# Sinkhorn block attention followed by a four-expert layer on one core: keys mixed and transposed in one matmul, attention output kept on chip, instruction order written by hand

## The chip, the cores and the metric

The kernel runs on one core of one Trainium2 chip. The time is the device time of one execution in microseconds (us). Of the kernel before there are three runs: 533.26, 534.28 and 534.55 us, median 534.28 us. One further execution was taken with the hardware profiler, and all durations below are from it.

## What is computed

There are 4 batches of 8 heads, 768 positions and a head dimension of 64. Positions form 8 blocks of 96. For each head an 8x8 matrix P is normalised five times by rows and columns. Keys and values are then mixed block by block with P, each block of queries attends to the mixed block at the same place, and all heads of a position, joined to 512 numbers, go through four experts whose outputs are weighted and added.

```python
for _ in range(5):
    P = exp(P - max(P));  P = P / sum(P, axis=-1);  P = P / sum(P, axis=-2)
k_sorted = einsum('bhij,bhjcd->bhicd', P, k_blocks)      # the same for v
attn = softmax(scale * q_block @ k_sorted_block.T) @ v_sorted_block
x = attn as [4*768, 512]
for e in range(4):
    out += p[:, e:e+1] * (relu(x @ w1[e]) @ w2[e])       # w1 512x1024, w2 1024x512
```

## The kernel before

All matmul operands are float16; inputs are cast from float32 by the loads. "Tile" means a named buffer, and two heads that share the 128 partitions are called a pair: there are 16 pairs, 4 to a batch.

*Start.* SyncE loads `sort_net` into `sn` (L89), and ScalarE and VectorE normalise it (L92 to L103). The 8x8 matrices go to DRAM and come back rearranged (`p_dram` L106, `rhsP` L110). A small matmul (L112) and a mask (L119) make from them a block-diagonal 128x128 matrix `bd` for 16 heads at a time.

*Mixing.* GpSimd loads all of k and v (`mixsrc`, L130). 48 matmuls of 512 columns with `bd` mix them (L140), VectorE copies each result out (L142, tiles `mo`, four buffers), and SyncE stores it to `ks_dram` or `vs_dram` (L143).

*Queries.* 32 loads of 96 KB (L156, issued by GpSimd), 6 transposes for each pair (L161) and a copy (L163) give `qT`.

*Attention, pair by pair* (L241 to L313). Mixed keys are read back from DRAM (L245), transposed (L250) and copied (L252); mixed values are read back (L260). Scores of two heads come from 16 matmuls (L276), ScalarE takes their exponential in halves of 384 columns (L283), 16 matmuls with the exponential as weights apply them to the values (L297; a column of ones gives the sum), VectorE divides (L303, L304), and SyncE stores the result to `x_dram` (L311).

*Experts* (`moe_block`, L184 to L234), batch by batch. The batch's 768 rows are read back from `x_dram` (L186), transposed (L191) and copied by ScalarE to `xT` (L192). For each expert, 16 results `ps_h` of 384 columns (4 matmuls each, L201) go through a Relu (L207), and then 6 results `ps_o` of 512 columns (8 matmuls each, L214) are scaled and added by VectorE (L224, L229). The last expert's sums are stored (L234).

*What sets the order.* The program gives pairs and blocks in order, with `moe_block(b-1)` behind the last pair of batch b, and a scheduler that knows dependences and buffers decides how they stand on each engine. PSUM is two pools of four one-bank buffers, `psA` for attention and `psM` for experts. GpSimd keeps eight loads in flight.

Of the kernel before, what the change touches and what calls it, by code (L numbers as in the profile page):

```python
# [9 lines left out]
F32 = mybir.dt.float32  # L11
F16 = mybir.dt.float16
AF = mybir.ActivationFunctionType
ALU = mybir.AluOpType


@with_exitstack
def kernel(
# [15 lines left out]
    NBLK = sort_net.shape[-1]  # L34
    BLK = S // NBLK
# [6 lines left out]
    NCH = (BLK * D) // 512  # L42
    NKC = Dm // P
    NFC = FF // P
    NTC = S // P
    NPAIR = GH // 2
    NPB = H // 2
    NSUB = S // P
    NHALF = 2
    HBL = S // NHALF  # L50

    consts = ctx.enter_context(tc.tile_pool(name="consts", bufs=1))
    dramp = ctx.enter_context(tc.tile_pool(name="dramp", bufs=1, space=bass.MemoryType.DRAM))
    small = ctx.enter_context(tc.tile_pool(name="small", bufs=1))
# [3 lines left out]
    def psa(shape, dtype, name):  # L58
        return psA.tile(shape, dtype, tag="ps", name=name)

    def psm(shape, dtype, name):
        return psM.tile(shape, dtype, tag="ps", name=name)

    p_dram = dramp.tile([GH, NBLK, NBLK], F16, name="p_dram")
    ks_dram = dramp.tile([GH, S, D], F16, name="ks_dram")
    vs_dram = dramp.tile([GH, S, D], F16, name="vs_dram")
    x_dram = dramp.tile([B, S, H, D], F16, name="x_dram")

    ident = consts.tile([P, P], F16, name="ident")
    make_identity(nc, ident)  # L70
    lhsT8 = consts.tile([NBLK, 16, NBLK], F16, name="lhsT8")
    nc.gpsimd.memset(lhsT8[:], 0.0)
    nc.gpsimd.affine_select(
        out=lhsT8[:], in_=lhsT8[:], compare_op=ALU.not_equal, fill=1.0,
        base=0, pattern=[[0, 16], [1, NBLK]], channel_multiplier=-1,
    )
    bdmask = consts.tile([P, 16, NBLK], F16, name="bdmask")
    nc.gpsimd.memset(bdmask[:], 1.0)
    nc.gpsimd.affine_select(
        out=bdmask[:], in_=bdmask[:], compare_op=ALU.is_ge, fill=0.0,  # L80
        base=7, pattern=[[8, 16], [0, NBLK]], channel_multiplier=-1,
    )
    nc.gpsimd.affine_select(
        out=bdmask[:], in_=bdmask[:], compare_op=ALU.is_ge, fill=0.0,
        base=0, pattern=[[-8, 16], [0, NBLK]], channel_multiplier=1,
    )

    sn = small.tile([GH, NBLK, NBLK], F32, name="sn")
    nc.sync.dma_start(sn[:], sort_net.rearrange("b h i j -> (b h) i j"))  # L89
    srow = small.tile([GH, NBLK, 1], F32, name="srow")  # L90
    scol = small.tile([GH, NBLK, 1], F32, name="scol")
    for it in range(5):  # L92
        nc.scalar.activation(sn[:], sn[:], AF.Exp, bias=0.0, scale=1.0)
        nc.vector.tensor_reduce(srow[:], sn[:], mybir.AxisListType.X, ALU.add)
        nc.vector.reciprocal(srow[:], srow[:])
        nc.vector.tensor_tensor(sn[:], sn[:], srow[:].broadcast_to([GH, NBLK, NBLK]), ALU.mult)
        nc.vector.tensor_reduce(scol[:], sn[:].rearrange("p i j -> p j i"), mybir.AxisListType.X, ALU.add)
        nc.vector.reciprocal(scol[:], scol[:])
        nc.vector.tensor_tensor(
            sn[:], sn[:],  # L100
            scol[:].rearrange("p j o -> p o j").broadcast_to([GH, NBLK, NBLK]),
            ALU.mult,
        )  # L103
    sn16 = small.tile([GH, NBLK, NBLK], F16, name="sn16")
    nc.vector.tensor_copy(sn16[:], sn[:])
    nc.scalar.dma_start(p_dram[:], sn16[:])  # L106
    bdts = []
    for m in range(2):
        rhsP = small.tile([NBLK, 16, NBLK], F16, name=f"rhsP_{m}")
        nc.scalar.dma_start(rhsP[:], p_dram[ds(16 * m, 16)].rearrange("g i j -> j g i"))  # L110
        ps_bd = psa([P, P], F32, f"ps_bd_{m}")
        nc.tensor.matmul(  # L112
            ps_bd[:],
            lhsT8.rearrange("jp g j -> jp (g j)"),
            rhsP.rearrange("jp g i -> jp (g i)"),
            start=True, stop=True,
        )
        bdt = small.tile([P, P], F16, name=f"bd_{m}")
        nc.vector.tensor_tensor(bdt[:], ps_bd[:], bdmask.rearrange("p g i -> p (g i)"), ALU.mult)  # L119
        bdts.append(bdt)  # L120

    qtp = ctx.enter_context(tc.tile_pool(name="qtp", bufs=NPAIR))
    wpool = ctx.enter_context(tc.tile_pool(name="wpool", bufs=1))

    with tc.tile_pool(name="mixsrc", bufs=1) as mixsrc, tc.tile_pool(name="mixout", bufs=4) as mixout:
        srcs = {}
        for m in range(2):
            for (tin, nm) in ((k, "k"), (v, "v")):
                src = mixsrc.tile([P, NCH, 512], F16, name=f"mixsrc_{nm}_{m}", tag=f"mixsrc_{nm}_{m}")
                nc.gpsimd.dma_start(  # L130
                    src.rearrange("p ch c -> p (ch c)"),
                    tin.rearrange("b h (j c) d -> (b h j) (c d)", j=NBLK)[ds(P * m, P), :],
                )
                srcs[(nm, m)] = src
        for m in range(2):
            for (tdr, nm) in ((ks_dram, "k"), (vs_dram, "v")):
                src = srcs[(nm, m)]
                for ch in range(NCH):
                    ps_mx = psa([P, 512], F32, f"ps_mx_{m}_{nm}_{ch}")
                    nc.tensor.matmul(ps_mx[:], bdts[m][:], src[:, ch, :], start=True, stop=True)  # L140
                    mo = mixout.tile([P, 512], F16, name=f"mo_{nm}_{m}_{ch}", tag="mo")
                    nc.vector.tensor_copy(mo[:], ps_mx[:])  # L142
                    nc.sync.dma_start(  # L143
                        tdr.rearrange("g (i ch cc) d -> (g i) ch cc d", ch=NCH, cc=8)[
                            ds(P * m, P), ch, :, :
                        ],
                        mo.rearrange("p (cc d) -> p cc d", cc=8),
                    )

        qTs = []  # L150
        with tc.tile_pool(name="qnp", bufs=4) as qnp:
            for pr in range(NPAIR):
                b, h2 = divmod(pr, NPB)
                q_nat = qnp.tile([P, NTC, 2, D], F16, name=f"q_nat_{pr}", tag="q_nat")
                for hh in range(2):
                    nc.gpsimd.dma_start(  # L156
                        q_nat[:, :, hh, :], q[b, 2 * h2 + hh].rearrange("(t p) d -> p t d", p=P)
                    )
                ps_qT = psa([P, NTC, P], F16, f"ps_qT_{pr}")
                for t in range(NTC):  # L160
                    nc.tensor.transpose(ps_qT[:, t, :], q_nat[:, t, :, :], ident[:])  # L161
                qT = qtp.tile([P, NTC, P], F16, name=f"qT_{pr}", tag="qT")
                nc.vector.tensor_copy(qT[:], ps_qT[:])  # L163
                qTs.append(qT.rearrange("dd t c -> dd (t c)"))
# [194 lines left out]
```

## Time and profile before

| what | value |
|---|---|
| profiled execution, first to last instruction | 532.5 us |
| median of three runs | 534.28 us |
| TensorE matmul busy | 417.9 us (78%) |
| VectorE busy | 160.8 us (30%) |
| ScalarE busy | 163.4 us (31%) |
| DMA moved | 43.50 MB in 125983 packets, 107008 of them under 512 bytes |
| first expert matmul on the chain that ended last | 171.85 us |
| end of that chain's last matmul | 528.39 us |

The profiled execution lies 1.8 us below the median of the runs. PE is TensorE, PEld its weight loads, DVE VectorE, ACT ScalarE, POOL GpSimd, SP SyncE; a "q" behind the name is the engine's own queue of DMA issues. A row of a group of instructions gives line, engine, operation, tiles written and read, shapes, count, then busy time, the mean duration of one in ns, and the engine's idle time before them with what ended it. A matmul's own duration holds the time until its result is written, so that matmuls in a stream overlap: what one costs in a stream is read from many of them, time by count.

### The profile page before, as it was taken

The numbers are of one execution on the slowest core, as the hardware profiler recorded it, in microseconds if no ns is written. First come the engines' busy times: TensorE is split into PE (matmuls) and PEld (weight loads), VectorE is DVE, ScalarE is ACT, GpSimd is POOL, SyncE is SP. The second block draws the span as 40 slices with busy tenths as digits, with TensorE's granted clock in tenths as the row PEclk, the third lists the DMA queues.
The fourth block names the chain that finished last, engine by engine and source line by source line (L and its number), as shares of the span: only waits on it lengthen the run. The fifth ranks groups of instructions, "written<-read, shape, count | busy, mean of one in ns | idle before, by whom it ended". The sixth has DMA issues, their size and how long they took to land.

```text
span 532.5 us, 6716 instructions
## 1 busy us (share of the span) xinstructions
PE 417.9 (78%) x2642; PEld 227.0 (43%) x2642; DVE 160.8 (30%) x341; ACT 163.4 (31%) x342; POOL 41.2 (8%) x87
## 2 busy tenths in 40 slices
PE   0003331464578999999999999999999999999996
PEld 0000000023466655545565554566555455455552
DVE  4102332583454331131533213153221311212213
ACT  1000000000135713514562351456235145252250
POOL 5114000029200000000000000000000000000000
PEclk9999999995555999999999999999999999999999
DMA  7999999879978900000571000144100012000003
GB/s 137 219 157 151 234 228 230 192 183 130 78 120 164 173 6 0 1 1 28 143 127 47 0 1 0 41 119 70 42 0 2 0 41 80 0 1 0 1 0 119
DMA packets 125983, 43.50 MB, mean 82 GB/s; under 512 B 107008, under 2 KB 120320, under 8 KB 125440
## 3 DMA queue, kind: packets, MB, share of 16 engines
q0 software_dynamic: 31936, 17.83, 26.9%
q1 hardware_dynamic: 85312, 15.80, 16.0%
q10 hardware_dynamic: 8704, 9.45, 6.0%
q8 instruction: 21, 0.34, 0.3%
q14 instruction: 10, 0.08, 0.0%
HBM read 45.15 MB, written 15.73 MB: 114 GB/s over the span
## 4 chain that ended last, share of the span: by engine, by line
PE 68%; ACT 3%; DMA 2%; DVE 1%; issue 0%; ACTq 0%
PE ps_o L214 31%; PE ps_h L201 31%; PE ps_av L297 2%; ACT ET L283 2%; DMA xnat<-x_dram 1%; PE ps_sT L276 1%; PE ps_kT L250 1%; PE ps_xT L191 1%; ACT xT L192 1%; DMA q_nat<-in_q_dram 1%; DVE kT L252 1%; DMA x_dram<-xsl 0%; PE ps_qT L161 0%; ACT hT L207 0%; DVE xsl L304 0%
## 5 line engine op out<-in xcount | busy, mean ns | idle before, releaser
L207 ACT ACTIVATE hT<-ps_h 128x384 f16<-128x384 f32 x256 | 124.5, 492 | 166.2 <-PE ps_h L201 164.1
L201 PE MATMUL ps_h<-xT,w 128*128 128x384 f16 x1024 | 173.9, 326 | 0.6 <-ACT xT L192 0.5
L214 PE MATMUL ps_o<-w,hT 128*128 128x512 f16 x768 | 168.4, 379 | 0.0
L201 PEld LDWEIGHTS <-w 128*128 128x128 f16 x1024 | 99.2, 98 | 66.2 <-issue 1.5
L214 PEld LDWEIGHTS <-hT 128*128 128x128 f16 x768 | 75.1, 98 | 89.0
L229 DVE SCALAR_TENSOR_TENSOR oacc<-ps_o,p_sb,oacc 128x512 f32<-128x512 f32 x72 | 54.1, 751 | 195.1 <-PE ps_o L214 195.1
L283 ACT ACTIVATE ET<-ps_sT 96x384 f16<-96x384 f32 x64 | 26.1, 492 | 154.1 <-PE ps_sT L276 154.0
L112 PE MATMUL ps_bd<-rhsP,lhsT 8*128 8x128 f16 x2 | 0.5, 259 | 46.7 <-DMA rhsP<-p_dram 46.7
L140 PEld LDWEIGHTS <-bd 128*128 128x128 f16 x48 | 5.1, 109 | 66.6 <-issue 66.6
L156 POOL DMA_DIRECT2D q_nat<-in_q_dram x32 | 26.3, 862 | 91.8 <-PE ps_qT L161 66.1
L224 DVE TENSOR_SCALAR oacc<-ps_o,p_sb 128x512 f32<-128x512 f32 x24 | 18.0, 751 | 45.5 <-PE ps_o L214 45.5
L140 PE MATMUL ps_mx_v<-mixsrc_v,bd 128*128 128x512 f16 x24 | 14.0, 585 | 20.2 <-DVE mo_v L142 14.4
L140 PE MATMUL ps_mx_k<-mixsrc_k,bd 128*128 128x512 f16 x24 | 13.1, 595 | 20.5 <-DVE mo_v L142 10.4
L304 DVE TENSOR_TENSOR xsl<-ps_av,rz 96x256 f16<-96x256 f32 x64 | 24.8, 408 | 0.9 <-DVE rz L303 0.3
L297 PE MATMUL ps_av<-vs,ET 96*96 96x65 f16 x256 | 21.3, 234 | 4.7 <-ACT ET L283 4.6
L142 DVE CAST mo_v<-ps_mx_v 128x512 f16<-128x512 f32 x24 | 15.9, 689 | 23.2 <-DMA vs_dram<-mo_v 18.2
L297 PEld LDWEIGHTS <-ET 96*96 96x96 f16 x256 | 18.3, 150 | 9.8 <-ACT ET L283 8.8
L161 PE MATMUL ps_qT<-ident,q_nat 128*128 128x128 f16 x96 | 12.0, 299 | 13.1 <-DMA q_nat<-in_q_dram 10.9
L261 POOL MEMSET vs<- 96x8 f16 x32 | 4.1, 133 | 217.9 <-PE ps_av L297 195.6
L142 DVE CAST mo_k<-ps_mx_k 128x512 f16<-128x512 f32 x24 | 15.7, 687 | 14.6 <-DMA ks_dram<-mo_k 13.1
L303 DVE RECIPROCAL rz<-ps_av 96x4 f32<-96x4 f32 x64 | 11.3, 176 | 28.4 <-PE ps_av L297 26.8
L192 ACT COPY xT<-ps_xT 128x768 f16<-128x768 f16 x16 | 11.9, 816 | 23.8 <-PE ps_xT L191 23.7
(39 smaller groups left out, 101.8 us busy)
## 6 DMA issues: line engine op xcount, KB each, us to landing
w<-in_moe_w_dram POOLq DMA_DIRECT2D x8, 1024.0 KB, 29.7
out_dram<-oacc ACTq DMA_DIRECT2D x24, 256.0 KB, 2.0
mixsrc_k<-in_k_dram POOLq DMA_DIRECT2D x2, 1536.0 KB, 17.8
mixsrc_v<-in_v_dram POOLq DMA_DIRECT2D x2, 1536.0 KB, 24.7
q_nat<-in_q_dram POOLq DMA_DIRECT2D x32, 96.0 KB, 3.9
ks_dram<-mo_k SPq DMA_DIRECT2D x24, 128.0 KB, 5.8
vs_dram<-mo_v SPq DMA_DIRECT2D x24, 128.0 KB, 3.0
ks_nat<-ks_dram SPq DMA_DIRECT2D x32, 96.0 KB, 2.9
```

The lines of the kernel that those rows point to most:

```text
L140: nc.tensor.matmul(ps_mx[:], bdts[m][:], src[:, ch, :], start=True, stop=True)
L142: nc.vector.tensor_copy(mo[:], ps_mx[:])
L156: nc.gpsimd.dma_start(q_nat[:, :, hh, :], q[b, 2 * h2 + hh].rearrange("(t p) d -> p t d", p=P))
L192: nc.scalar.copy(xT[:, u, :], ps_xT[:])
L201: nc.tensor.matmul(ps_h[:], w1sb[e][:, kc, ds(fc * P, P)], xT[:, kc, ds(nh * HBL, HBL)], start=(kc == 0), stop=(kc == NKC - 1),)
L207: nc.scalar.activation(hT[:, fc, ds(nh * HBL, HBL)], ps_h[:], AF.Relu, bias=0.0, scale=1.0)
L214: nc.tensor.matmul(ps_o[:], hT[:, fc, ds(ns * P, P)], w2sb[e][:, fc, :], start=(fc == 0), stop=(fc == NFC - 1),)
L224: nc.vector.tensor_scalar(out=oacc[:], in0=ps_o[:], scalar1=pcol, scalar2=None, op0=ALU.mult)
L229: nc.vector.scalar_tensor_tensor(out=oacc[:], in0=ps_o[:], scalar=pcol, op0=ALU.mult, in1=oacc[:], op1=ALU.add,)
L283: nc.scalar.activation(ETs[hh][:, ds(half * 4, 4), :], pshh[hh][:, :, 0:96], AF.Exp, bias=0.0, scale=SCALE,)
L297: nc.tensor.matmul(ps_av[:, ii, 0:D + 1], ET[:, i, :], vs_sb[:, i, 0:D + 1], start=True, stop=True,)
L304: nc.vector.tensor_tensor(xsl[:, ds(half * 4, 4), :], ps_av[:, :, 0:D], rz[:, ds(half * 4, 4), :].broadcast_to([96, 4, D]), ALU.mult,)
```

## The change

*Layout.* A partition holds 6 consecutive positions of a head (`load_natural`, rows of 6x64 numbers), so that 16 partitions make one block of 96. k, v and q of a batch are three tiles, loaded for 4 or 8 heads at a time. The order of positions inside a block is the same everywhere and is put back by the store of the output.

*Mixing.* The 8x8 matrices don't go to DRAM. 8 small matmuls spread them over partitions (`ps_R`), and a mask times a row of them gives for each head a 128x128 block-pattern matrix: `PIv` and `PIk` (`build_PI`; four heads at a time, the first four on VectorE, the rest on GpSimd). `st_v` mixes values with `PIv` as weights, copies them to `vo`, and takes them through DRAM once (`vs_dram`) in quads of heads. `st_k` uses the natural keys as weights and `PIk` as moving operand, so its result is already mixed and transposed: 12 matmuls of 64 weight columns for each pair. `st_q` transposes queries in 12 pieces of the same form. `st_x` transposes the attention output from on-chip tiles into `xT`; `ks_dram` and `x_dram` are gone.

*Sizes.* Scores and exponentials are taken for 768 columns of a head at once, Relu for 768 columns. A PSUM tile is now two banks, two buffers in each of the two pools. Score and value matmuls load 128 weight columns (32 of them beyond the block).

*Order.* The scheduler is off: every engine runs its instructions as the program gives them. Batch 0's attention stands ahead of the experts. In `experts(b)`, the 24 steps of batch b+1's attention (4 each of v, q, k, s, a, x) are put behind expert results, one at a time, spread over 50 of the 56 results. The last batch's experts have none.

```diff
-    psA = ctx.enter_context(tc.tile_pool(name="psA", bufs=4, space=bass.MemoryType.PSUM))
-    psM = ctx.enter_context(tc.tile_pool(name="psM", bufs=4, space=bass.MemoryType.PSUM))
+    ctx.enter_context(tc.manual_schedule())
...
+    psA = ctx.enter_context(tc.tile_pool(name="psA", bufs=2, space=bass.MemoryType.PSUM))
+    psM = ctx.enter_context(tc.tile_pool(name="psM", bufs=2, space=bass.MemoryType.PSUM))
...
+    def load_natural(b, nm, lo, n):
...
+        nc.gpsimd.dma_start(
+            t[:, ds(lo, n), :, :].rearrange("p h r d -> p h (r d)"),
+            src[b, ds(lo, n)].rearrange("h (p r) d -> p h (r d)", r=R),
+        )
...
+    for lo in range(0, H, 4):
+        for nm in ("k", "v", "q"):
+            load_natural(0, nm, lo, 4)
...
+    load_w1(0)
+    load_w2(0)
...
-    nc.scalar.dma_start(p_dram[:], sn16[:])
-        nc.scalar.dma_start(rhsP[:], p_dram[ds(16 * m, 16)].rearrange("g i j -> j g i"))
+    for i in range(NB):
+        nc.tensor.matmul(
+            ps_R[:, i, :],
+            sn16[:, i, :, :].rearrange("g j c -> g (j c)"),
+            ident[0:GH, 0:GH],
+            start=True, stop=True,
+        )
+    nc.vector.tensor_copy(Rs[:], ps_R.rearrange("p i g -> p g i"))
...
+    build_PI(nc.vector, 0, "v")
+    build_PI(nc.vector, 0, "k")
+    build_PI(nc.gpsimd, 1, "v")
+    build_PI(nc.gpsimd, 1, "k")
+    load_w1(1)
+    load_w2(1)
+    for nm in ("k", "v", "q"):
+        load_natural(1, nm, 0, H)
+    for n in range(2, GH // 4):
+        build_PI(nc.gpsimd, n, "v")
+        build_PI(nc.gpsimd, n, "k")
+    for e in range(2, E):
+        load_w1(e)
+        load_w2(e)
...
+    def st_v(b, pr):
+        ps = psa([P, 2, 512], F32, f"ps_v_{b}_{pr}")
...
+        if pr % 2:
+            nc.sync.dma_start(
+                vs_dram[b, qd].rearrange("r c i x -> (c i) r x"),
+                vo.rearrange("p r h w -> p r (h w)"),
+            )
...
+            nc.sync.dma_start(
+                vs.rearrange("c i h w -> c (i h w)"),
+                vs_dram[b, qd].rearrange("r c i x -> (r c) (i x)"),
+            )
...
+    def st_k(b, pr):
+        ps = psa([P, R, P], F32, f"ps_k_{b}_{pr}")
+        for r in range(R):
+            for hh in range(2):
+                nc.tensor.matmul(
+                    ps[ds(D * hh, D), r, :],
+                    natural[(b, "k")][:, h, r, :],
+                    PIk[(b * H + h) // 4][:, h % 4, :, :].rearrange("p i c -> p (i c)"),
...
+    def attention_order(b):
+        o = [(st_v, 0), (st_v, 1), (st_q, 0), (st_k, 0), (st_v, 2), (st_v, 3)]
+        for pr in range(NPB):
+            o.append((st_s, pr))
+            if pr + 1 < NPB:
+                o += [(st_q, pr + 1), (st_k, pr + 1)]
+            o.append((st_a, pr))
+            o.append((st_x, pr))
+        for pr in range(NPB - 1):
+            o.remove((st_x, pr))
+            o.insert(o.index((st_s, pr + 1)) + 1, (st_x, pr))
...
+    def experts(b, filler):
+        slots = E * (NFC + R)
+        def slot():
+            done[0] += 1
+            while fill and done[1] < (done[0] * (len(filler))) // (slots - 6):
+                fill.pop(0)()
+                done[1] += 1
...
+    for f in attention_order(0):
+        f()
+    for b in range(B):
+        if b + 2 < B:
+            for nm in ("k", "v", "q"):
+                load_natural(b + 2, nm, 0, H)
+        experts(b, attention_order(b + 1) if b + 1 < B else [])
```

VectorE at the end of the normalisation, in the kernel before: `sn` and `scol` belong to it, `sn16` is its result, `bd` the block-diagonal matrix, `mo_k` the mixed keys on their way to DRAM.

```order
L98 RECIPROCAL scol_90<-scol_90 32x8
L99 TENSOR_TENSOR sn_87<-sn_87,scol_90 32x64
L105 CAST sn16_126<-sn_87 32x64
L119 TENSOR_TENSOR bd_0_133<-ps_bd_0_131,bdmask_83 128x128
L119 TENSOR_TENSOR bd_1_139<-ps_bd_1_137,bdmask_83 128x128
L142 CAST mo_k_0_0_163<-ps_mx_0_k_0_161 128x512
L142 CAST mo_k_0_1_168<-ps_mx_0_k_1_166 128x512
```

And at the same place in the changed kernel, where `Rs` is the spread of the 8x8 matrices and `PIv_0`, `PIk_0` are the patterns of the first four heads.

```order
L145 RECIPROCAL scol_129<-scol_129 32x8
L146 TENSOR_TENSOR sn_80<-sn_80,scol_129 32x64
L152 CAST sn16_165<-sn_80 32x1024
L165 CAST Rs_176<-ps_R_167 128x256
L180 TENSOR_TENSOR PIv_0_186<-maskv_108,Rs_176 128x512
L173 TENSOR_TENSOR PIk_0_178<-maskk_106,Rs_176 128x512
L217 CAST vo_0_122<-ps_v_0_0_224 128x6x2x64
L217 CAST vo_0_122<-ps_v_0_1_228 128x6x2x64
L242 COPY qT_0_0_248<-ps_q_0_0_235 128x768
L257 CAST kT_0_110<-ps_k_0_0_250 128x768
```

What stood between the normalisation and the first mixed tile was the trip of `sn16` through DRAM, which VectorE's `bd` waits for; now four VectorE operations and the `ps_R` matmuls stand there, and the copies of one batch's attention follow, not those of all mixed keys.

ScalarE where attention of a later pair meets the experts, in the kernel before: `hT` is the Relu's output from `ps_h`, `ET` the exponential from the scores `ps_sT`.

```order
L207 ACTIVATE hT_0_0_1302<-ps_h_0_0_0_0_1303 128x384
L207 ACTIVATE hT_0_0_1302<-ps_h_0_0_0_1_1309 128x384
L283 ACTIVATE ET_14_1205<-ps_sT_7_0_0_1207 96x384
L283 ACTIVATE ET_15_1206<-ps_sT_7_1_0_1208 96x384
L283 ACTIVATE ET_14_1205<-ps_sT_7_0_1_1219 96x384
L283 ACTIVATE ET_15_1206<-ps_sT_7_1_1_1220 96x384
L207 ACTIVATE hT_0_0_1302<-ps_h_0_0_1_0_1315 128x384
L207 ACTIVATE hT_0_0_1302<-ps_h_0_0_1_1_1321 128x384
```

And in the changed kernel, at the first score step inside an expert (batch 0's expert 1).

```order
L371 ACTIVATE hT_0_0_595<-ps_h_0_0_7_692 128x768
L371 ACTIVATE hT_0_1_793<-ps_h_0_1_0_794 128x768
L274 ACTIVATE ET_0_114<-ps_s_1_0_0_804 96x768
L274 ACTIVATE ET_1_116<-ps_s_1_0_1_805 96x768
L371 ACTIVATE hT_0_1_793<-ps_h_0_1_1_824 128x768
L371 ACTIVATE hT_0_1_793<-ps_h_0_1_2_834 128x768
```

Each operation covers two of the old ones, and two exponentials stand between two Relus whose `ps_h` buffers are the only two there are.

More of the change, by code (lines that the diff above doesn't have):

```diff
@@ L14 @@
 ALU = mybir.AluOpType
+AX = mybir.AxisListType
 @with_exitstack
@@ L117 @@
         )
[L118 to L132, printed above, removed]
-                )
[L134 to L164, printed above, removed]
@@ L184, in moe_block @@
[L184 to L194 removed]
+    Rs = const.tile([P, GH, NB], F16, name="Rs")
@@ new lines, in st_x @@
+    def st_x(b, pr):
+        if b not in xTs:
+            xTs[b] = moe.tile([P, NKC, R, NB, CP], F16, name=f"xT_{b}", tag="xT")
+        ps = psa([P, NB, BLK], F16, f"ps_x_{b}_{pr}")
+        xsl = xsls[(b, pr)]
+        for i in range(NB):
+            nc.tensor.transpose(
+                ps[:, i, :], xsl[:, i, :, :].rearrange("c h d -> c (h d)"), ident[0:BLK, 0:BLK]
+            )
+        nc.vector.tensor_copy(
+            xTs[b][:, pr, :, :, :].rearrange("p r i c -> p i r c"),
+            ps.rearrange("p i (r c) -> p i r c", c=CP),
+        )
```

385 lines of the change are left out of this document (200 added, 185 removed).

## The prediction

> **What bounds the kernel now.** I read the page's slices first, then the chain that ended last, then busy time by stretch, then the timeline of the start. The slices show two kernels behind each other.
>
> ```profile
> PE   0003331464578999999999999999999999999996
> PEclk9999999995555999999999999999999999999999
> DMA  7999999879978900000571000144100012000003
> ```
>
> A slice is 13.3 us. From slice 13 (173 us) on, TensorE is full; ahead of that the DMA engines are full and TensorE is not. The chain, whose rows give start, length and work, says the same.
>
> ```profile
> 144.48 0.66 PE ps_kT L250 x6
> 148.83 0.65 PE ps_kT L250 x6
> 159.24 2.15 DMA x_dram<-xsl
> 161.56 6.30 DMA xnat<-x_dram
> 171.85 0.69 PE ps_h L201 x4
> 195.60 10.40 PE ps_h L201 x64
> 206.00 10.36 PE ps_o L214 x48
> 528.39 0.03 issue
> 528.41 0.75 DVE oacc L229
> ```
>
> The first expert matmul stands at 171.85 us. An expert on one batch takes 10.40 + 10.36 = 20.76 us, 16 of them 332.2 us; A matmul of 384 columns takes 10.40/64 = 162.5 ns there and one of 512 takes 10.36/48 = 215.8 ns, in streams without holes. From 171.85 to 528.39 are 356.5 us, so attention and waits add only 24.3 us there. The time to be had is ahead of 171.85, and the timeline shows what it goes into.
>
> ```profile
> 6.73 0.20 DVE L94 TENSOR_REDUCE srow<-sn 32x8 f32<-32x64 f32 x1
> 15.24 0.18 DVE L105 CAST sn<-sn 32x64 f16<-32x64 f32 x1
> 42.12 0.26 PE L112 MATMUL ps_bd<-rhsP,lhsT 8*128 8x128 f16 x1 [42.12 <-DMA rhsP<-p_dram]
> 47.12 1.46 PE L140 MATMUL ps_mx_k<-mixsrc_k,bd 128*128 128x512 f16 x3
> 53.00:66.00 13.00, 3.78 (x7) 0.73 (x7) 4.84 (x7) 0.00 (x0) 0.00 (x0) 1.00 1.12 234
> 160.00:164.00 4.00, 2.99 (x34) 2.52 (x36) 2.48 (x9) 1.21 (x4) 0.26 (x2) 0.50 0.71 110
> 168.00:172.00 4.00, 4.00 (x46) 3.61 (x47) 0.28 (x2) 2.81 (x6) 0.00 (x0) 0.52 0.91 142
> ```
>
> (The last three: stretch, length, busy PE, PEld, DVE, ACT, POOL with counts, granted clock, DMA share, GB/s.) The 8x8 matrices are done at 15.4 us, but the matmul that needs them waits for their trip through DRAM until 42.12. Then mixing goes at the pace of stores and loads: 3.78 us of 13 on TensorE, DMA full at 234 GB/s.
>
> **The start (T0, the first expert matmul).** Loads: batch 0 needs 24 heads' worth of 96 KB, 2.36 MB in float16. In before, the first loads ran as here:
>
> ```profile
> mixsrc_k<-in_k_dram POOLq DMA_DIRECT2D x2, 1536.0 KB, 17.8
> 13.30:26.60 13.30, 0.00 (x0) 0.00 (x0) 1.59 (x8) 0.26 (x1) 1.64 (x2) 1.00 1.04 218
> 124.00:128.00 4.00, 1.59 (x12) 1.12 (x12) 1.67 (x3) 0.00 (x0) 4.00 (x6) 0.50 1.97 127
> ```
>
> At 218 GB/s batch 0 takes 11 us and the first expert's two weights (2.1 MB) 10 more: there at about 25 us. The new rows are 768 bytes in float16; the q loads of 128 bytes made 127 GB/s, by which it would be 19 and 35 us. Neither end is late for T0. Behind them come expert 1's weights and batch 1 (at 218 GB/s by 46 us), then 4.2 MB more by 65, needed from T0 + 40 on. GpSimd issues them behind pattern builds; those 14 builds of 512 columns have no row on GpSimd. VectorE would take 0.67 us for one (worked out below), and three times that, 2 us, would still have the last load issued by 50 us.
>
> Chain to the first mix: VectorE begins the normalisation once the identity is built behind six load issues. A big load's issue took 0.55 to 0.71 us, so about 5.5 us against 6.73, done near 14.5. Then `sn16` for 1024 columns, eight tiny matmuls, `Rs`, `PIv`. For sizes the trace lacks I take the slope between sizes:
>
> ```profile
> L142 DVE CAST mo_v<-ps_mx_v 128x512 f16<-128x512 f32 x24 | 15.9, 689 | 23.2 <-DMA vs_dram<-mo_v 18.2 <-DMA ks_dram<-mo_k 3.6 <-PE ps_mx_v L140 1.4
> L304 DVE TENSOR_TENSOR xsl<-ps_av,rz 96x256 f16<-96x256 f32 x64 | 24.8, 408 | 0.9 <-DVE rz L303 0.3
> L303 DVE RECIPROCAL rz<-ps_av 96x4 f32<-96x4 f32 x64 | 11.3, 176 | 28.4 <-PE ps_av L297 26.8
> L252 DVE COPY kT<-ps_kT 128x768 f16<-128x768 f16 x16 | 8.7, 541 | 6.0 <-PE ps_kT L250 5.7
> L99 DVE TENSOR_TENSOR sn<-sn,scol 32x64 f32<-32x64 f32 x5 | 1.1, 212 | 0.2
> ```
>
> A cast goes from 0.18 us for 64 columns (the 15.24 row) to 0.689 for 512: 1.13 ns a column, so 1.27 us for 1024, 0.40 for 256, 0.98 for 768. A product goes from 212 to 408 ns over 192 columns: 0.67 us for 512. Sum 1.27 + 0.7 (matmuls and handing over) + 0.40 + 0.67 + 0.25 = 3.3: first mix at 17.8 us. Nothing waits for DRAM.
>
> Batch 0's attention, four pairs with no experts to hide it. VectorE a pair: two casts of 768 (v, k) 1.96, two float16 copies (q, x) 1.10, two divisions of 176 ns and two products 1.70: 4.8 us, 19 us for four. TensorE at half clock (the 0.50 of the row 160 to 164): before's own cold rows give the prices.
>
> ```profile
> 148.64 0.83 PE L250 MATMUL ps_kT<-ident,ks_nat 128*128 128x128 f16 x6
> 150.12 0.88 PE L276 MATMUL ps_sT<-qT,kT 64*96 64x96 f16 x16 [0.65 <-DVE kT L252]
> 147.66 1.17 PE L297 MATMUL ps_av<-vs,ET 96*96 96x65 f16 x12 [0.23 <-ACT ET L283]
> L283 ACT ACTIVATE ET<-ps_sT 96x384 f16<-96x384 f32 x64 | 26.1, 492 | 154.1 <-PE ps_sT L276 154.0
> L192 ACT COPY xT<-ps_xT 128x768 f16<-128x768 f16 x16 | 11.9, 816 | 23.8 <-PE ps_xT L191 23.7
> ```
>
> Without the last one's 0.2 us of completion: 6 transposes in 0.65 (108 ns each), 16 scores in 0.63 (39 ns), 12 value matmuls in 0.97 (81 ns). So a pair takes v 0.65, q and k 12 each at 54 to 108 ns, scores 0.63, values 1.3, x 0.65: 4.5 to 5.8, four pairs 18 to 23 us. Both engines are near 20 us and take turns; I take 22, plus 4 us of unshared beginning and end (two exponentials of about 0.82 us each, as the 816 ns row has for 768 columns; the last pair's division, transpose and copy), plus 2 for the values' trip through DRAM, which is issued after the second v step and needed some 8 us later, while a store under load took
>
> ```profile
> ks_dram<-mo_k SPq DMA_DIRECT2D x24, 128.0 KB, 5.8
> vs<-vs_dram SPq DMA_DIRECT2D x32, 96.0 KB, 2.7
> out_dram<-oacc ACTq DMA_DIRECT2D x24, 256.0 KB, 2.0
> ```
>
> 5.8 and a read 2.7 us. Its wait would sit on TensorE's queue ahead of the first value step, with all later scores behind it. T0 = 17.8 + 28 = 46; bounds 38 (VectorE's 19 alone) and 56 (serial q and k, 5 us more for values). Granting full clock takes a full stretch such as 168 to 172, so I add 2 us.
>
> **The experts.** 332.2 us of matmuls stay, in the same shapes. The steps of 12 pairs lie between them on TensorE, and none of their streaming can be hidden. Warm prices:
>
> ```profile
> 268.09 0.69 PE L297 MATMUL ps_av<-vs,ET 96*96 96x65 f16 x12
> 268.61 0.50 PE L250 MATMUL ps_kT<-ident,ks_nat 128*128 128x128 f16 x6
> 270.34 0.56 PE L276 MATMUL ps_sT<-qT,kT 64*96 64x96 f16 x16
> 270.83 0.34 PE L201 MATMUL ps_h<-xT,w 128*128 128x384 f16 x1
> ```
>
> Start to start, 12 value matmuls take 0.52 us (43 ns), 6 transposes 0.34 (57 ns for 128 columns), 16 scores 0.49 (31 ns, where 57 ns for 128 columns would make 43 for 96: two heads in two row halves of the array overlap in part). q and k use two column halves, which no row shows: between half of 57 and 57 ns. I take the scores' share, 57 x 31/43 = 41 ns, so 12 make 0.49 us. Values stream 65 columns, 29 ns by columns and 43 as before: I take 37, 0.6 us. v is two of 162.5 ns, 0.33, x eight of 43, 0.34. A pair: 0.33 + 0.49 + 0.49 + 0.49 + 0.6 + 0.34 = 2.74 us; with all cheap ends 2.3, with all dear ends 3.2. 12 pairs: 33 us, 28 to 39.
>
> Waits. A step comes every second or third expert result, 2.6 us or more, and the longest answer it needs is VectorE's 1.7 us for a division of both heads. Two exponentials (1.64 us) delay one Relu (about 0.81 us for 768 columns) while TensorE fills the other `ps_h` buffer in 1.30 us: the Relu ends 2.6 us after the scores do, the buffer is wanted at 2.6. I take 3 us for all, 0 to 12. ScalarE's and VectorE's sums (124.5 us of Relu at two for one, under 80 us of attention copies) don't come near the stretch.
>
> The last product, the store (2.0 us) and the end stay as they are: 532.5 - 528.4 = 4.1.
>
> Sum: 46 + 2 + 332.2 + 33 + 3 + 4.1 = 420.3 us; with the 1.8 us by which the median lies above the profiled execution, **422 us**. Ends: 38 + 332.2 + 28 + 4.1 + 1.8 = 404, and 56 + 2 + 332.2 + 39 + 12 + 4.1 + 1.8 = 447.
>
> **Rivals.** *The array pays for each change of form* (0.15). Every q, k and s step goes from the full array to halves and back: 3 x 2 x 12 = 72 changes. If each emptied the array, it would cost what a matmul's result lags behind its column stream, 326 - 162 = 164 ns by the group row:
>
> ```profile
> L201 PE MATMUL ps_h<-xT,w 128*128 128x384 f16 x1024 | 173.9, 326 | 0.6 <-ACT xT L192 0.5
> ```
>
> That is 12 us, and q and k without overlap 5 more (24 x 16 ns x 12): 439. Against it stands the row at 270.34: the scores with both changes took 0.49 us, less than the 0.69 of their columns one by one. [...]
>
> *The start stays with its transfers* (0.14). Loads at 127 GB/s and a values trip like the wait for `rhsP` hold T0 at about 64, or the first v step of batch 1 inside expert 0 (its values would be there at 64 too, 8.1 MB): 440. For it: DMA stays full to 65 us. Against: rows of 768 and 528 bytes, not 16 and 128.
>
> *The start goes warm* (0.10). If batch 0's attention is dense enough for the full clock, TensorE is off its path: T0 40, no 2 us, and with cheap steps 409. The 160 to 164 row speaks against: 75% busy and still 0.50. [...]
>
> *Steps wait in the stream* (0.05). In order, any late copy stops the experts: 0.5 us at each of 72 steps gives 458.
>
> *Slower: the experts run cold* (0.02). If waits at the steps leave TensorE about 75% busy, as from 160 to 164, the clock stays at half. Each us of the 365 done cold costs one more; 112 us of them, 31%, bring it back to 534, and the three batches with steps (249 + 33 = 282 us) would give 704. It needs 1.3 us of waiting at each of 72 steps, a third of the 3.9 us of work between two.
>
> **How the numbers follow.** The forecast has 0.54: 411 to 434. The range 404 to 448 reaches from the cheap ends to the dear ones and takes in the first three rivals; the last two, 0.07, are left out. Less than 0.3% is what a measurement here can't tell from no change. Faster 0.97, same 0.01, slower 0.02.
>
> **What would show it.** First expert matmul near 46 us; no wait on TensorE for `rhsP`-like transfers; a pair's steps at 2.7 us; TensorE at 1.00 and above 97% busy from 50 us; last matmul near 416. Wrong: clock 0.50 after 60 us, PE waiting for ACT at `ps_h` or for DMA at `ps_v`, or a first `ps_h` after 60.

## The result, and the profile after

The changed kernel takes 432.03 us (median of four runs, 431.29 to 432.24) against 534.41 us: a ratio of 0.8083, 95% interval 0.8067 to 0.8099. The forecast was 422. Two executions of the runs below took far longer than the others of their kernel (836 us of x2_sp, 1424 us of x11_nohold) and are left out of its time. The profiled execution of the changed kernel has a span of 429.6 us and took 432.24 us in all.

The slices of the page (10.7 us each now), in the same three rows as ahead of the prediction:

```profile
PE   0321889999999999999999999999999999999995
PEclk9975569999999999999999999999999999999999
DMA  9999999940009422200000221200000300000003
```

Counted from 0, TensorE is full from slice 6 on (64 us), where it was full from slice 13 of longer ones (173 us). What stands ahead of it is a dip: 3, 2, 1 in slices 1 to 3, with DMA full. The chain that ended last says what the dip is (start, length, work):

```profile
15.63 0.69 DVE sn L152
17.26 0.43 DVE PIv L180
19.14 1.74 DVE vo L217 x2
20.96 13.06 DMA vs_dram<-vo
...
34.45 9.93 DMA vs_dram<-vo
44.40 5.91 DMA vs<-vs_dram
50.35 0.64 PE ps_a L288 x8
56.79 5.99 PE ps_h L365 x24
142.89 10.36 PE ps_o L379 x48
237.26 10.36 PE ps_o L379 x48
```

The first mix starts at 17.74 us as forecast. Then the mixed values' store takes 13.06 us, the second quad's 9.93, and expert matmuls start at 56.79. From there on every batch with steps takes 237.26 - 142.89 = 94.4 us. The table of waits shows that nothing else counts (TensorE's longest rows: total, times, longest; two more have 0.2 us each):

```profile
PE ps_R L158 <- DVE sn L152: 16.4, 1, 16.4
PE ps_a L288 <- DMA vs<-vs_dram: 16.2, 2, 15.7
PE ps_x L310 <- DVE xsl L297: 3.6, 4, 1.4
PE ps_v L210 <- DVE PIv L180: 1.0, 1, 1.0
```

All of these lie ahead of 56.8 us; the first is the time in which the 8x8 matrices are made, when TensorE has no other work. Inside the expert stream TensorE waits for nobody, and the row by stretch has it busy for all 94.35 us of a batch, at full clock:

```profile
153.25:247.60 94.35, 94.35 (x714) 51.30 (x712) 36.16 (x56) 31.28 (x40) 0.00 (x0) 1.00 0.11 35
```

So the 102.9 us between the two spans come from the start: the first expert matmul moved from 171.85 to 56.79 us, 115.1 us. The stretch from there to the last matmul (425.07) grew from 356.5 to 368.3: all of three batches' attention now lies in it, mixing and queries included, where in the kernel before 144 of the 256 score matmuls lay in it and no mixing. The tail is the same within 0.4 us.

Some steps of batch 2's attention in the stream, from the chain:

```profile
177.74 0.45 PE ps_s L267 x16
178.18 2.71 PE ps_h L365 x16
180.89 0.46 PE ps_q L238 x12
181.34 2.71 PE ps_h L365 x16
...
194.74 0.34 PE ps_x L310 x8
195.08 5.18 PE ps_o L379 x24
...
206.58 0.48 PE ps_a L288 x16
207.07 2.60 PE ps_h L365 x16
```

16 expert matmuls of 384 columns take 2.60 us behind an a step; behind s, q and k they take 2.71. Behind an x step they take the usual time too (24 of 512 columns in 5.18 us, 216 ns each). That 0.11 us is looked at below.

### The profile page after: what moved, and what is told of

It reads as the page before. It is cut to its first block, busy times and chain, and to the rows that moved or that the text cites. A ratio compares the mean times of both kernels' runs of the same rounds, so it can differ in the third digit from the quotient of the medians.

```text
span 429.6 us, 6396 instructions
## 1 busy us (share of the span) xinstructions
PE 387.3 (90%) x2856; PEld 212.8 (50%) x2856; DVE 155.4 (36%) x265; ACT 128.3 (30%) x166; POOL 35.1 (8%) x51
## 4 chain that ended last, share of the span: by engine, by line
PE 86%; DMA 7%; DVE 4%; POOL 1%; issue 1%; ACT 0%; SPq 0%; POOLq 0%
PE ps_h L365 40%; PE ps_o L379 39%; DMA vs_dram<-vo 5%; PE ps_a L288 2%; DMA vs<-vs_dram 1%; PE ps_x L310 1%; PE ps_q L238 1%; PE ps_k L250 1%; PE ps_s L267 1%; PE ps_v L210 1%; DVE xsl L297 1%; DVE vo L217 0%; POOL nat_k L84 0%; POOL nat_v L84 0%; DVE PIk L173 0%
## 5 line engine op out<-in xcount | busy, mean ns | idle before, releaser
L371 ACT ACTIVATE hT<-ps_h 128x768 f16<-128x768 f32 x128 | 103.8, 811 | 237.8 <-PE ps_h L365 237.8
L274 ACT ACTIVATE ET<-ps_s 96x768 f16<-96x768 f32 x32 | 24.0, 802 | 37.8 <-PE ps_s L267 37.8
L288 PE MATMUL ps_a<-vs,ET 96*128 96x65 f16 x256 | 12.0, 206 | 16.2 <-DMA vs<-vs_dram 16.2
L297 DVE TENSOR_TENSOR xsl<-ps_a,rz 96x512 f16<-96x512 f32 x32 | 22.0, 687 | 1.1
L217 DVE CAST vo<-ps_v 128x768 f16<-128x768 f32 x16 | 15.1, 950 | 17.6 <-PE ps_v L210 17.6
L313 DVE COPY xT<-ps_x 128x768 f16<-128x768 f16 x16 | 8.9, 556 | 34.2 <-PE ps_x L310 34.2
L257 DVE CAST kT<-ps_k 128x768 f16<-128x768 f32 x16 | 15.2, 953 | 15.4 <-PE ps_k L250 15.2
L288 PEld LDWEIGHTS <-ET 96*128 96x128 f16 x256 | 11.1, 106 | 18.6 <-issue 16.0
L158 PE MATMUL ps_R<-ident,sn 32*128 32x32 f16 x8 | 0.4, 185 | 16.4 <-DVE sn L152 16.4
L310 PE MATMUL ps_x<-ident,xsl 96*128 96x96 f16 x128 | 9.3, 224 | 3.6 <-DVE xsl L297 3.6
L267 PE MATMUL ps_s<-qT,kT 64*128 64x96 f16 x256 | 9.5, 222 | 0.3 <-DVE kT L257 0.2
## 6 DMA issues: line engine op xcount, KB each, us to landing
nat_k<-in_k_dram POOLq DMA_DIRECT2D x3, 768.0 KB, 23.3
```

Source lines behind the costliest of these rows:

```text
L217: nc.vector.tensor_copy(vo[:, :, ds(2 * (pr % 2), 2), 0:D], ps[:, :, 0:R * D].rearrange("p h (r d) -> p r h d", r=R),)
L257: nc.vector.tensor_copy(kT[:, 0:S].rearrange("p (i r c) -> p i r c", i=NB, r=R), ps.rearrange("p r (i c) -> p i r c", c=CP),)
L267: nc.tensor.matmul(pss[hh][:, i // HB, ds((i % HB) * BLK, BLK)], kT[ds(D * hh, D), ds(i * BLK, P)], qT[ds(D * hh, D), i, :], start=True, s ...
L274: nc.scalar.activation(ETs[2 * (pr % 2) + hh][:, 0:S].rearrange("c (a x) -> c a x", a=2), pss[hh][0:BLK, :, 0:HS], AF.Exp, bias=0.0, scale ...
L288: nc.tensor.matmul(ps[:, i // HB, ds((i % HB) * VW, D + 1)], ET[:, ds(i * BLK, P)], vs[:, i, 2 * (pr % 2) + hh, 0:D + 1], start=True, stop ...
L297: nc.vector.tensor_tensor(xsl[:, :, hh, :].rearrange("c (a i) d -> c a i d", a=2), av[:, :, :, 0:D], rz[:].broadcast_to([BLK, 2, HB, D]), ...
```

## The experiments

Eleven runs. The wait in the third column is TensorE's wait for the first values (`vs`); T0 is the first expert matmul, as the timeline has it; the chain, where a piece begins when the one before has ended, has it 0.2 us later (56.79 us for the changed kernel).

| run | T0, us | wait, us | time, us | ratio to before, 95% interval |
|---|---|---|---|---|
| changed kernel | 56.6 | 15.7 | 432.03 | 0.8083 (0.8067 to 0.8099) |
| x1_hold | 47.8 | 7.1 | 430.91 | 0.8082 (0.8061 to 0.8103) |
| x2_sp | 57.2 | 16.9 | 431.92 | 0.8098 (0.8086 to 0.8111) |
| x4_byhead | 56.0 | 14.8 | 437.37 | 0.8196 (0.8181 to 0.8211) |
| x6_qk | 55.9 | 14.9 | 429.22 | 0.8046 (0.8035 to 0.8057) |
| x9_front | 45.5 | 4.9 | 417.64 | 0.7823 (0.7811 to 0.7835) |
| x7_xdram | 90.2 | 15.3 | 493.89 | 0.9251 (0.9230 to 0.9272) |
| x5_twofirst | 93.9 | 15.2 | 457.21 | 0.8570 (0.8557 to 0.8583) |
| x8_sched | 52.7 | 12.5 | 428.66 | 0.8030 (0.8015 to 0.8045) |
| x11_nohold | 44.9 | 5.4 | 417.92 | 0.7841 (0.7826 to 0.7856) |
| x10_snfirst | 42.3 | 7.1 | 415.54 | 0.7799 (0.7785 to 0.7813) |
| x12_clear | 41.0 | 4.9 | 413.88 | 0.7756 (0.7741 to 0.7771) |

### The slow trip: loads, queue order, or short rows?

**x1_hold.** GpSimd's later loads wait for batch 0's values, and all its pattern builds come ahead of them.

```diff
+    nc.gpsimd.tensor_copy(hold[:], vss[(0, 1)][:, 0, 0, 0:2])
     load_w1(1)
     load_w2(1)
     for nm in ("k", "v", "q"):
         load_natural(1, nm, 0, H)
...
```

> Expert 1 to 3's weights and batch 1's k, v and q are issued only once batch 0's values are back from DRAM (a small GpSimd copy reads them first); GpSimd's pattern builds come ahead of that. The changed kernel has its first expert matmul at 56.8 us, a store of values that takes 13.1 us and a wait of 15.7 us on TensorE. Theory A (the trip is slow because the bulk loads fill the DMA engines): the stores land in 3 to 5 us, the wait falls to 5 us or less, the first expert matmul comes at 42 to 46 us, and the time falls from 432 to 418 to 423. Theory B (the second quad's store stands on SyncE's queue behind the first quad's read, so two trips run one behind the other): the wait is one of order, the stores still take about 10 us, and the time stays within 4 us of 432. Theory C (rows of 528 bytes are slow by themselves): as B, the stores stay at 10 us or more.

Its chain and its waits:

```profile
20.96 6.99 DMA vs_dram<-vo
28.38 4.56 DMA vs_dram<-vo
32.96 3.84 DMA vs<-vs_dram
39.65 19.30 DMA nat_v<-in_v_dram
```

```profile
PE ps_a L292 <- DMA vs<-vs_dram: 7.1, 1, 7.1
PE ps_v L214 <- DMA nat_v<-in_v_dram: 5.8, 1, 5.8
```

The stores went from 13.06 and 9.93 us to 6.99 and 4.56, the wait from 15.7 to 7.1, and T0 by 9 us. So the loads are the cause of the slow trip, and short rows are not (theory C falls). The stores didn't reach the 3 to 5 us expected of theory A: expert 0's second weight, issued at 7.64 us in the changed kernel, wasn't held, and by my estimate the DMA engines were full until about 26 us (2.36 MB of batch 0 and 2.1 MB of weights at the 199 to 207 GB/s that the changed kernel moved from 4 to 16 us). And the time moved by only 1 us where 9 to 14 were expected: batch 1's v, held behind 2 MB of weights and batch 1's k, lands at 59 us, TensorE waits 5.8 us for it inside expert 0, and the 16 expert matmuls behind the wait take 4.84 us instead of 2.60, 302 ns each instead of 162.5. A wait was removed and another took its place.

**x2_sp.** Both stores ahead of both reads, for batch 0.

```diff
-            vs = att.tile([BLK, NB, 4, VW], F16, name=f"vs_{b}_{qd}", tag="vs")
...
-                vs_dram[b, qd].rearrange("r c i x -> (r c) (i x)"),
+            for qr in ([qd] if b else [0, 1] if qd else []):
+                vs = att.tile([BLK, NB, 4, VW], F16, name=f"vs_{b}_{qr}", tag="vs")
...
+                    vs_dram[b, qr].rearrange("r c i x -> (r c) (i x)"),
```

> For batch 0 alone SyncE issues both quads' stores ahead of both reads; nothing else is changed. Theory A (bulk loads): the first value step still waits about 15 us, since its own trip isn't shortened, and the time stays within 3 us of 432, or rises by up to 3, the two stores sharing the engines. Theory B (queue order): the second trip ends some 10 us earlier, the first expert matmul comes near 47 us and the time falls to about 422.

```profile
PE ps_a L289 <- DMA vs<-vs_dram: 16.9, 1, 16.9
```

The time is that of the changed kernel. SyncE's order costs nothing by itself: in the changed kernel the second quad, read 10 us after the first, was waited for by no more than 0.5 us (16.2 in two waits, 15.7 the longest), and here the first quad's read runs beside the second's, takes 7.40 us and is waited for 1.2 us longer. Theory B falls.

**x9_front.** Only expert 0's first weight is loaded ahead; then the hold; then batch 1's v, expert 0's second weight, batch 1's q and k, and the other weights. Four more pattern builds come ahead of the held loads, the rest behind them. Stores as in x2_sp, q and k together as in x6_qk.

```diff
     load_w1(0)
-    load_w2(0)
...
+    nc.gpsimd.tensor_copy(hold[:], vss[(0, 1)][:, 0, 0, 0:2])
+    load_natural(1, "v", 0, H)
+    load_w2(0)
+    load_natural(1, "q", 0, H)
+    load_natural(1, "k", 0, H)
+    for e in range(1, E):
+        load_w1(e)
+        load_w2(e)
```

> Three things at the start and one in the stream: only expert 0's first weight stands ahead of the hold; both quads' stores go ahead of both reads on SyncE; the loads held until batch 0's values are back come in the order batch 1's v, expert 0's second weight, batch 1's q and k, then the other weights; and q and k steps are merged as in the run that took 429.2 us. Theory A (bulk loads slow the trip, and holding them only moved the wait to batch 1's v because that load was late): stores 3 to 5 us, the first wait on TensorE about 4 us, no wait for batch 1's v, first expert matmul at 41 to 45 us, time 414 to 419. If the trip is slow for another reason too, or the held loads come late wherever they stand: 424 or more, with a wait for a load inside the first expert.

417.64 us, inside what theory A gave; T0, 45.5 us, lies just above its 41 to 45. Of the 14.4 us, q and k together are worth 2.8 (x6_qk) and the order of the stores nothing (x2_sp), so that about 11.6 belong to the loads and builds. No wait for a load is left in the stream; the first wait and the chain at its end:

```profile
PE ps_a L296 <- DMA vs<-vs_dram: 4.9, 1, 4.9
```

```profile
24.40 4.83 DMA vs<-vs_dram
29.36 0.61 PE ps_a L296 x8
45.71 6.18 PE ps_h L379 x24
```

**x11_nohold.** The same without the `tensor_copy` that holds the loads.

> The run that took 417.6 us without its hold: GpSimd issues the same loads in the same order as soon as its pattern builds let it (near 24 us), and nothing waits for batch 0's values. Theory A (the bulk loads are what slows the trip): the first store, issued at 21 us, still lands in 4 us, the second store and both reads meet the loads and take 6 to 13 us, the wait on TensorE goes from 4.9 to 9 to 14 us and the time to 422 to 428. If the order of stores and reads or of the loads was what helped: within 2 us of 417.6.

417.92 us: the hold itself is worth nothing measurable, against what I expected of theory A. The stretch from 20 to 24 us shows why, first in the changed kernel, then here (the last two numbers are the DMA share and GB/s):

```profile
20.00:24.00 4.00, 3.49 (x46) 2.04 (x43) 4.00 (x7) 0.89 (x2) 4.00 (x6) 1.00 1.20 197
```

```profile
20.00:24.00 4.00, 3.19 (x46) 1.81 (x43) 4.00 (x7) 1.06 (x2) 4.00 (x5) 1.00 0.43 117
```

The store is issued at 21 us in both. In x11 expert 0's second weight isn't in flight and GpSimd is busy with pattern builds until 24.0 us, so the store finds the DMA engines nearly empty (no slice reaches a share of 0.1 from 20.5 to 21.8 us in x9_front, whose start is the same); in the changed kernel they are full (1.22 from 21 to 22 us). What decided it was what the engines have in hand when the first store and its read are issued, and moving one weight and the builds was enough: the loads that GpSimd issues from 24.0 us on, just ahead of the read at 24.4, made the read 5.32 us long instead of 4.83. Which of the two moves counts for more wasn't tested singly. Batch 1's store in x9_front, issued under the loads at 57.1 us, again took 13.1 us to the read's issue, and nothing waited for it, because it lies in the stream.

**x10_snfirst.** x9_front, and VectorE starts the normalisation ahead of the masks, which wait for the identity matrix.

```diff
-    eye16 = const.tile([P, CP], F16, name="eye16")
-    nc.vector.tensor_reduce(eye16[:], ident.rearrange("p (j c) -> p c j", c=CP), AX.X, ALU.max)
...
+    eye16 = const.tile([P, CP], F16, name="eye16")
+    nc.vector.tensor_reduce(eye16[:], ident.rearrange("p (j c) -> p c j", c=CP), AX.X, ALU.max)
...
     ps_R = psa([P, NB, GH], F32, "ps_R")
```

> The run that took 417.6 us with one more change at the start: VectorE begins the normalisation at once and prepares the masks behind it, where it waited for the identity matrix until 6.5 us. The first mix comes about 3.5 us earlier (17.7 to 14.2 us: 4.4 us of earlier start, 0.8 us of mask work, half of it hidden by the small matmuls), everything behind it moves along, and the time falls to about 414, if batch 0's loads and the first store don't meet expert 0's first weight. If they do, the trip takes up to 4 us more and the time stays near 417.6.

415.54 us, between the two values. The first mix came at 13.46 us instead of 17.7, but the store, now issued at 16.7, met the first weight's load (a DMA share of 1.11 from 16 to 20 us), took 6.76 us to the read's issue, and the wait grew:

```profile
PE ps_a L296 <- DMA vs<-vs_dram: 7.1, 1, 7.1
```

**x12_clear.** x10_snfirst with that weight as the first of the held loads.

```diff
-    load_w1(0)
...
     nc.gpsimd.tensor_copy(hold[:], vss[(0, 1)][:, 0, 0, 0:2])
+    load_w1(0)
     load_natural(1, "v", 0, H)
```

> The run that took 415.5 us with expert 0's first weight held too, as the first of the held loads. There the first store of values, issued at 16.7 us, met that weight's load, and TensorE waited 7.1 us. Theory A, as the run without a hold left it (what counts is what the DMA engines have in hand when the store is issued): the store lands in about 3.5 us, the wait falls to 3 to 5 us, the first expert matmul comes near 39 us, the weight is there by 32 us, and the time falls by 2 to 4 us, to 411.5 to 413.5. If the trip has a floor of its own near 10 us, or the weight now comes late: 415 or more.

413.88 us, 0.4 us above the expected range, T0 41.0 where 39 was expected, and the weight there near 36 us instead of 32, still ahead of T0; the wait fell as stated:

```profile
PE ps_a L295 <- DMA vs<-vs_dram: 4.9, 1, 4.9
```

```profile
20.16 4.84 DMA vs<-vs_dram
25.14 0.61 PE ps_a L295 x8
41.19 5.18 PE ps_h L378 x24
```

The store (issued at 16.7) had landed by 20.1, and the trip still takes 8.3 us in all, with nothing but the two quads' stores and reads and, from 24.05 us on, a load of 48 KB moving, of which 4.9 are waited for. In the remaining 16 us to T0 TensorE and VectorE take turns at four pairs: from 26 to 40 us they are busy 10.2 and 10.7 of 14 us, TensorE at half clock for most of it (granted clock 0.6 in the page's slices from 20.6 to 41.1 us). This version beats the changed kernel by 18 us and takes 22.4% less than the kernel before.

### What the steps in the stream cost

**x4_byhead.** All matmuls of one head ahead of the other's.

```diff
-        for r in range(R):
-            for hh in range(2):
+        for hh in range(2):
+            for r in range(R):
```

(in the q and k steps; in the s step with blocks `i` for `r`.)

> In the q, k and s steps all matmuls of one head come ahead of all of the other, where the changed kernel takes the heads in turn. If two heads overlap in the halves of the array, this takes it away: q and k go from 0.46 to about 0.68 us (12 at 57 ns), s from 0.45 to about 0.69 (16 at 43 ns), 0.7 us a pair, 8 us for the 12 pairs inside the experts, and the time rises to about 440. If there is no overlap and the steps are short for another reason, the time stays within 2 us of 432.

437.37 us, 5.3 more: the direction of overlap, two thirds of its size. The chain has the steps at

```profile
164.63 0.59 PE ps_q L238 x12
168.35 0.59 PE ps_k L250 x12
179.64 0.63 PE ps_s L267 x16
```

0.13 to 0.18 us above those shown of the changed kernel. The heads do overlap when taken in turn; why q and k by head they lose 0.13 and not 0.22 us isn't settled.

**x6_qk.** q and k step of a pair side by side in the stream.

```diff
+            if f is st_k:
+                steps[-1] = steps[-1] + [(f, pr)]
```

> The q and the k step of a pair are put into the expert stream together, so that the array goes from full to halves and back once for both. In the trace of the changed kernel expert matmuls after a q, k or s step take 0.11 us more than those after v, a or x. If that 0.11 us is a price of the change of form, 12 of 36 visits go and the time falls by 1.3 us, to 430.7 (0.3%). If it belongs to the step's own matmuls, the time stays within 0.5 us of 432.

429.22 us, 2.8 less, more than either expected case. Its chain:

```profile
162.89 0.46 PE ps_q L238 x12
163.35 0.34 PE ps_k L250 x12
163.68 3.56 PE ps_o L385 x16
```

The k step fell from 0.46 to 0.34 us when a q step stands ahead of it, and one of the two 0.11 us behind the steps is gone: 0.23 us a pair. A batch takes 93.52 us instead of 94.37 (235.00 - 141.48 in its chain), 0.85 for four pairs, 2.6 for three batches; the rest goes with an earlier T0 (55.9 us). So the price of a change of form is about 0.11 us going in and 0.11 coming back, and 12 matmuls without it take 0.34 us, 28 ns each, half of the 57 that one of 128 columns takes: full overlap. What happens in the array at such a change the traces don't show.

### What the parts are worth

**x7_xdram.** The attention output goes through DRAM again: a store for each pair in place of its transposes, eight reads behind the last pair, and then six transposes and a copy for each 128 columns of the model width. (Here and in x5_twofirst the expert outputs have 7 buffers and not 9, for room.)

```diff
+        nc.sync.dma_start(
+            x_dram[b, :, :, ds(pr * P, P)].rearrange("i c x -> c i x"),
+            xsls[(b, pr)].rearrange("c i h d -> c i (h d)"),
+        )
+        if pr == NPB - 1:
...
+            for i in range(NB):
+                nc.sync.dma_start(
+                    xn[ds(i * CP, CP), :, :],
+                    x_dram[b, i].rearrange("(r c) x -> c r x", c=CP),
+                )
```

> One part undone: the attention output of a batch goes to DRAM pair by pair, is read back as 128 rows of 512, transposed in 24 pieces and copied to the experts' operand, as the kernel before does (7 accumulators' buffers in place of 9 make room). Theory: for batch 0 the trip stands alone on the path, 8.5 us as in the kernel before or up to 20 under the bulk loads; for batches 1 to 3 the last pair's trip comes too late for the end of the stream and TensorE waits 3 to 6 us each time: 450 to 470. If the output's way through DRAM hides in the stream: only batch 0's part shows, 438 to 448.

```profile
PE ps_x L324 <- DMA xn<-x_dram: 54.7, 4, 31.4
```

493.89 us, 62 more and dearer than I expected. Batch 0's trip under the loads is waited for 31.4 us, the other three 23.3 together. Keeping the output on chip is worth these 62 us in this order, 54.7 of them this wait: far more than the 8.5 us that the trip took in the kernel before. It isn't the cost of such a trip in itself: batch 0's runs under the loads, and the others' reads are issued behind their batch's last pair, shortly ahead of the steps that need them.

**x5_twofirst.** Batch 1's attention ahead of the experts too.

```diff
-    for f in attention_order(0): f()
+    for b in range(2):
+        for f in attention_order(b): f()
...
-        experts(b, attention_order(b + 1) if b + 1 < B else [])
+        experts(b, attention_order(b + 2) if b + 2 < B else [])
```

> Batch 1's attention stands ahead of the experts too, and batch b+2's goes into batch b's experts, so that one batch's attention is taken out of the stream (three buffers for the experts' operand, 7 accumulators' buffers). Inside the stream a batch's attention costs 11.3 us. Alone, at the pace of the trace's pairs at the start (5.0 us from 41.2 to 45.9 to 51.3 us), it takes about 20: the time rises by 7 to 12, to 439 to 444. If attention alone is no dearer than in the stream, it stays within 2 us of 432.

457.21 us, 25 more where 7 to 12 were expected. The chain shows the part that I left out:

```profile
58.95 12.18 DMA vs_dram<-vo
71.56 9.98 DMA vs_dram<-vo
81.62 5.99 DMA vs<-vs_dram
94.09 5.08 PE ps_h L365 x24
```

Batch 1's values make the same slow trip, now in the open: 15 us more of waiting. The other 22 us that T0 moved by are what a batch's attention costs alone, twice the 11.3 us that it costs in the stream.

**x8_sched.** The scheduler orders the same program.

```diff
-    ctx.enter_context(tc.manual_schedule())
```

> The hand-written order is given up: the scheduler of the kernel before orders the changed kernel's program, from the same program text. It puts the steps at nearly the same places (a few pulled into the middle of an expert result). If the gain comes from what the program text puts next to what, the time stays within 3 us of 432; if from the exact order on each engine, it rises by 5 or more.

428.66 us, 3.4 below the hand-written order, just beyond the 3 us expected of the first case and to the better side. It lets VectorE start the normalisation without waiting for the identity matrix (TensorE's wait for `sn16` is 13.5 us, not 16.4), and T0 is 52.7, 3.9 us earlier. A batch in the stream takes the same 94.37 us (234.28 - 139.91 in its chain); batch 0's is about 1 us longer, with a wait of 0.7 us for batch 1's q. The gain of the change isn't in the exact order, which loses a little, but in what the program puts beside what.

Two parts of the gain were not undone singly: the 8x8 matrices that no longer go through DRAM, and the keys mixed and transposed in one matmul. Together they moved the first mix from 47.12 to 17.74 us and took the stores and reads of mixed keys away; how that divides between them isn't shown.

## Why the prediction was right

The gain and its place were as stated, and its size within a tenth: 102 us where 112 were forecast. The sum was 10 us too low. One term, the values' trip, was 14 us too low; the four pairs at the start and the steps in the stream were 5 us too high together, and small terms 1 us too low. That the time lay no farther off is luck. Of the signs that the prediction named, three failed with that term: the first expert matmul near 46 us, no wait of TensorE for a transfer, and the last matmul near 416 us (it ended at 425.07). A pair's steps at 2.7 us came near (2.83), and TensorE was full, though from 60 us on and not from 50 (busy 365.00 us from 60 to 425, clock 1.00).

*The first mix at 17.8 us* came at 17.74, by luck: two errors cancel. These VectorE rows of the timeline have the identity matrix at 6.47 where 5.5 was taken, and the cast of 1024 columns at 0.68 us where 1.27 was:

```profile
6.47 0.38 DVE L109 TENSOR_REDUCE eye<-ident 128x16 f16<-128x128 f16 x1 [6.47 <-POOL ident masks.py:199]
15.63 0.68 DVE L152 CAST sn<-sn 32x1024 f16<-32x1024 f32 x1
...
17.26 0.43 DVE L180 TENSOR_TENSOR PIv<-maskv,Rs 128x512 f16<-128x512 f16 x1
17.60 1.54 DVE L173 TENSOR_TENSOR PIk<-maskk,Rs 128x512 f16<-128x512 f16 x1
```

*Batch 0's attention, 28 us, T0 46* is the step that failed in size. The term "plus 2 for the values' trip" was 16.2 us of waiting, 15.7 of them at one time. I had priced the store by the 5.8 us of a `ks_dram` store, though the loads that the change puts at that very place were in my own list. Without the wait the four pairs took 56.8 - 17.7 - 16.2 = 22.9 us, 3 less than the 26 of the sum. The bound of 56, which had 5 us more for the trip and dear matmuls, missed T0 by less than 1 us, and for the wrong reason; the lower bound of 38 should have been 17.8 + 19 = 36.8, and 16 scores at half clock are 0.68 us by their row (0.88 less 0.2), not 0.63; the first moves the lower end of the range by 1.2 us, the second the sum by 0.2.

*Cold start, 2 us*: 24 expert matmuls took 5.99 us instead of 3.90, so 2.1. The granted clock was 0.50 from 56 to 60 us, 0.89 from 60 to 64 and 1.00 from 64 to 84; in the kernel before it was 0.50 from 167.90 to 171.50 us, TensorE busy all through, and 1.00 from 172 to 180.

*A pair's steps, 2.74 us, and 3 us of waits*: (94.37 - 83.04)/4 = 2.83 us a pair, where 83.04 is four experts at 20.76, and no waits: 34 us for 12 pairs against 36 in the sum. Its parts were off both ways: q and k overlap fully (28 ns, taken as 41) and pay 0.22 us for the two changes of form, which I had given to a rival. Value matmuls took 30 ns, the cheap end.

*Tail and what lies around the span*: 4.1 and 1.8 us were 4.5 and 2.6.

Of the rivals, "the start stays with its transfers" came nearest, with T0 between forecast (46) and rival (64): the values' trip was slow, though because of the loads around it and not of its short rows, and the loads themselves were in time (the engines moved 207 to 227 GB/s in slices 1 to 7). "The array pays for each change of form" was right that each change costs time, 0.11 us for each of 72, 8 us, where it had 12; that a change empties the array no run shows. Full overlap paid back two thirds of that: without the changes each of the 36 q, k and s steps takes 0.34 us (measured for k; for q and s an estimate, 0.46 and 0.45 less 0.11) where 0.49 was in the sum, 5.4 us. "The start goes warm" began: a q step took 0.85 us at 19.14 and 0.62 at 23.12, and TensorE's granted clock fell only in the wait, from 0.85 (24 to 28 us) to 0.50. "Steps wait in the stream" and "slower" had no trace at all.

## What to carry to other kernels

When a phase's small transfer stands on the critical path, look at what the DMA engines have in hand at the moment it is issued; here moving one bulk load (expert 0's second weight) and some pattern builds was worth about 11 us, reordering every engine 3. The same 13 us trip costs nothing once it lies in a stream of other work, so put round trips there and keep them out of the start; where the result is wanted right behind them, they are waited for again (x7_xdram). And check a removed wait for the next one: the first hold made T0 9 us earlier and the kernel 1 us faster.

## What the runs showed of the hardware

A 396 KB store of 528-byte rows, from its issue to the read's, takes at most 3.5 us alone (16.70 to 20.16 in x12_clear, where the read's issue stands behind the second store's) and 13.1 under bulk loads, and its read 3.7 (x10_snfirst) to 7.4 (x2_sp). Matmuls of 64 weight columns in alternate halves of the array take 28 ns for 128 columns, half of 57, and entering and leaving such a form costs 0.11 us each way in a full stream (x6_qk). Value matmuls of 65 columns take 30 ns with 128 weight columns, and took 43 with 96 in the kernel before.

VectorE's product of 512 columns took 0.43 us for `PIv` and 1.54 us for `PIk` (the 17.26 and 17.60 rows above). Beside the second GpSimd ran two builds of its own, at 17.31 us for 1.28 and at 18.56 for 1.49, where its builds without VectorE's products beside them took 1.04 to 1.11. Whether the two engines hold each other up, and by what, isn't shown: the two products differ in their operands' layout too, and in all eight kernels whose timeline has both engines there VectorE's second one ran beside a GpSimd build.
